# Sixteen weight offsets, five matmul orders and three woven blocks in an attention and two-layer expert kernel

## The chip, the cores and the metric

The kernel runs on one core of a Trainium2 chip. The metric is the device time of one execution in microseconds; of several executions the median is taken. The core's engines run beside each other: TensorE (PE, with its weight loads shown as PEld), VectorE (DVE), ScalarE (ACT), GpSimd (POOL), and SyncE, whose queue issues nearly all DMAs.

## The reference

Attention with mixed heads is followed by two feed-forward layers, all in fp32. With 2 batches, 12 heads, a sequence of 448 and a head size of 64 the attention gives 896 rows of 768, and each feed-forward part widens them to 2048 and back:

```python
scores = scale * np.matmul(q, k.transpose(0, 1, 3, 2))
scores = np.einsum('bhij,hg->bgij', scores, w_pre)
attn = softmax(scores)
attn = np.einsum('bhij,hg->bgij', attn, w_post)
x = np.matmul(attn, v)                        # -> 896 x 768

h = x @ w_in                                  # 768 -> 2048
g = h * np.clip(h + 3.0, 0.0, 6.0) / 6.0
x = g @ w_out                                 # 2048 -> 768

h = x @ w_in2
g = np.maximum(h, 0.0) + alpha * np.minimum(h, 0.0)
return g @ w_out2
```

## The kernel before

The attention fills the first part of the span, the feed-forward layers the rest; their first matmuls lie among the last ones of the attention. Only the feed-forward layers are touched by the change.

Each number of these layers is held as a pair, a high part `h` in the type fp32r and a low part `l`, the rest. A product of two such pairs is three matmuls (`mm3`): high weights by high input, high weights by low input, low weights by high input. Each matmul has 128 rows, 128 columns of weights, and moves 448 columns (`S`), one of the two batch halves `c`. It brings its own weight load.

The weights come in 64 blocks of 128 x 768. Blocks 0 to 15 are the first input layer, 16 to 31 the first output layer, 32 to 47 the second input layer, 48 to 63 the second output layer. A block of an input layer holds one slice `f` of 128 hidden units, with six slices `kk` of the 768 inputs; `in_chain` adds 18 matmuls into one PSUM tile `p` for each half `c`. A block of an output layer holds two hidden slices by 384 outputs and adds 36 matmuls into six tiles. So every block is 36 matmuls, and the second input layer's block 32 starts at 414.78 us of the span.

A block arrives in a packed form of two 32-bit words per weight, and every engine has a share in unpacking it, for block `i` in this order:

- `load_w`: SyncE's queue brings `wst`.
- `conv_magnitude`: ScalarE makes `wb` from one word (L361) and scales the other (L367).
- `conv_shift`: VectorE clamps and shifts `wb` (L377, L378); `conv_sign`: VectorE puts the sign in (L385).
- `conv_round`: GpSimd adds the other word (L392).
- `conv_hi`: ScalarE casts `wb` to `whi` (L397); `conv_lo`: GpSimd subtracts to get `wlo` (L403).

There is no scheduler: each engine works in the order in which the code is written. In step `i` of an input layer `in_layer` writes: rounding for block i+2, the load for i+4, magnitude for i+3, then for half 0 the 18 matmuls, the activation, `conv_hi` and `conv_lo` for i+2 and `conv_shift` for i+3, and for half 1 the 18 matmuls, `conv_sign` for i+3 and the activation. The second layer's activation `act2` is two VectorE operations that read `p` (L505, L506), a cast on ScalarE (`gh`, L510) and a subtraction on VectorE (`gl`, L512). `whi` and `wlo` have three buffers each; `p` rotates over eight PSUM tiles.

In the built program every `whi` and `wlo` tile begins 192 bytes past a multiple of 256, and every slice that the matmuls move begins on a multiple of 256; the slices of the weights are 512 bytes apart.

Of the kernel before, what the change touches and what calls it, by code (L numbers as in the profile page):

```python
# [7 lines left out]
F32 = mybir.dt.float32  # L8
R = mybir.dt.float32r
# [4 lines left out]
ALU = mybir.AluOpType  # L14
# [21 lines left out]
def kernel(  # L36
# [15 lines left out]
    nc = tc.nc  # L52
    _, D, H, S = k.shape
    B, D = q.shape[0], D // 2
# [3 lines left out]
    KF = alpha.shape[0] // 128  # L58
    KD = DM // 128
# [10 lines left out]
    for b in range(B):  # L70
        for i0 in range(0, S, GP):
            n = min(GP, S - i0)
# [34 lines left out]
    with tc.manual_schedule():  # L107
# [214 lines left out]
        for ti in range(NTILE - 1):  # L322
            lo = (tiles[ti]["s"] + tiles[ti]["ng"] - 1) // 2 + 2
            hi = tiles[ti + 2]["s"] // 2 + 1 if ti + 2 < NTILE else lo + 4
# [3 lines left out]
        P = {}  # L328
        WC = w_in1.shape[2]
        blocks = []  # L330
# [3 lines left out]
        st_t, b_t, w_t, x_t, x_whole = {}, {}, {}, {}, {}  # L334
# [22 lines left out]
        def conv_abs(i):  # L357
            if i < len(blocks):
                t = w_tile(i, "wb", [128, WC], F32)
                s = st_t[i]  # L360
                nc.scalar.activation(t, s[:, :, 1].bitcast(F32), ACTF.Abs)  # L361
                b_t[i] = t

        def conv_low(i):
            if i < len(blocks):
                s = st_t[i]
                nc.scalar.activation(s[:, :, 0].bitcast(I32), s[:, :, 0], ACTF.Copy, scale=2.0 ** -29)  # L367

        def conv_magnitude(i):
            conv_abs(i)  # L370
            conv_low(i)

        def conv_shift(i):
            if i < len(blocks):
                t = b_t[i]
                u = t.bitcast(U32)
                nc.vector.tensor_scalar(t, t, W_MAX, W_MIN, ALU.min, ALU.max)  # L377
                nc.vector.tensor_scalar(  # L378
                    u, u, 3, 0x3FFFFFFF, ALU.logical_shift_left, ALU.bitwise_and
                )  # L380
# [8 lines left out]
        def conv_round(i):  # L389
            if i < len(blocks):  # L390
                n = b_t[i].bitcast(I32)
                nc.gpsimd.tensor_tensor(n, n, st_t.pop(i)[:, :, 0].bitcast(I32), ALU.add)  # L392

        def conv_hi(i):
            if i < len(blocks):
                hi = P["w"].tile([128, WC], R, tag="whi", bufs=3, name="whi")
                nc.scalar.copy(hi, b_t[i])  # L397
                w_t[i] = [hi]

        def conv_lo(i):  # L400
            if i < len(blocks):
                lo = P["w"].tile([128, WC], R, tag="wlo", bufs=3, name="wlo")
                nc.gpsimd.tensor_tensor(lo, b_t.pop(i), w_t[i][0].bitcast(F32), ALU.subtract)  # L403
                m = KD if blocks[i][0] == "in" else 2
                w_t[i] = [x.rearrange("p (k f) -> p k f", k=m) for x in (w_t[i][0], lo)]

        def conv_a(i):
            conv_magnitude(i)
# [29 lines left out]
        def ptile():  # L438
            if "ps6" not in P:
                return P["ps2"].tile([128, 512], F32, tag="p", name="p")  # L440
            n_ps[0] += 1
            where = P["ps6"] if n_ps[0] % 8 < 6 else P["ps2"]
            return where.tile([128, 512], F32, tag="p", name="p")
# [24 lines left out]
        def mm3(p, wt, xt, first, last):  # L468
            for z, (a, c) in enumerate(((0, 0), (0, 1), (1, 0))):
                nc.tensor.matmul(  # L470
                    p, wt[a], xt[c], start=(first and z == 0), stop=(last and z == 2)
                )

        def in_part(p, i, xs, c, k0, k1):
            for kk in range(k0, k1):
                mm3(p, [w[:, kk, :] for w in w_t[i]], xs[kk, c], kk == 0, kk == KD - 1)

        def in_chain(i, xs, c):
            p = ptile()[:, :S]
            in_part(p, i, xs, c, 0, KD)  # L480
            return p

        def g_tile(f, c):
            return pair(P["g0" if c == 0 and f < NE else "g1"], "g")
# [29 lines left out]
        def run(a):  # L514
            for _ in a:
                pass

        def in_layer(i, xs, act, gs, f0):
            for f in range(f0, KF):
                conv_round(i + 2)  # L520
                load_w(i + 4)
                conv_magnitude(i + 3)
                for c in range(B):
                    p = in_chain(i, xs, c)
                    gs[f, c] = g_tile(f, c)
                    a = act(p, gs[f, c], f)
                    next(a)
                    if c == 0:
                        conv_hi(i + 2)
                        conv_lo(i + 2)  # L530
                        conv_shift(i + 3)
                        next(a)
                    else:
                        conv_sign(i + 3)
                        next(a)
                    run(a)
                w_t.pop(i)
                i += 1
            return i
# [11 lines left out]
        for c in range(2):  # L551
            a = GH * c
# [24 lines left out]
        for i in range(NC):  # L577
            a = 2 * (17 + 7 * i)
# [35 lines left out]
        for p_ in range(-2, NP + 1):  # L614
            if p_ == -2:
                for g in range(6):
                    if g == 4:
                        for c in range(2):
                            a = GH * c
# [35 lines left out]
            kk = 2 * (p_ - (NP - KD // 2))  # L655
# [36 lines left out]
        for f in range(NC):  # L692
            p = in_chain(f, x_t, 1)
# [134 lines left out]
```

## Time and profile before

| | |
|---|---|
| time, median of 3 runs | 647.37 us |
| time, lowest and highest run | 644.71 and 649.35 us |
| span of the profiled execution | 649.1 us |
| TensorE busy | 634.1 us, 98% of the span |
| VectorE, ScalarE, GpSimd busy | 64%, 53%, 45% of the span |
| granted TensorE clock | 1.000 |

The span runs from the first to the last instruction of one profiled execution; the runs are other executions of the same kernel. The profiled one lies 1.7 us above the median of the runs and within what they span. The clock of 1.000 is the upper of TensorE's two levels, 2.4 GHz. Busy shares are means over stages that differ much, so they don't say what sets the end.

### The profile page before, as it was taken

To read this page: it belongs to the slowest core of one execution; us is meant where nothing else is said; L and a number is where in the kernel's file an instruction comes from. 1 tells how busy PE (TensorE), PEld (TensorE's weight loads), DVE (VectorE), ACT (ScalarE), POOL (GpSimd) and SP (SyncE) were. 2 spreads that over 40 slices of the span, in tenths; PEclk is the share of its full clock that TensorE was granted. 3 is DMA by queue.
4 is the path that set the end of the run, shared out by engine and by line. 5 is a ranking of instruction groups with operands and counts; after the bars stand their busy time and mean duration, and the time that the engine had idled before them with its cause. 6 is when DMAs were issued, how large, how long until landed. Compare 5 with 4: busy or idle time off the path is not lost.

```text
span 649.1 us, 16015 instructions
## 1 busy us (share of the span) xinstructions
PE 634.1 (98%) x6696; PEld 545.8 (84%) x6696; DVE 417.6 (64%) x649; ACT 344.0 (53%) x635; POOL 294.2 (45%) x240
## 2 busy tenths in 40 slices
PE   7999999899899999999999999999999999999997
PEld 2667666666589999999999999999999999999997
DVE  3866666668546888887534634489999997454401
ACT  4877778686555566656444433444444443444310
POOL 4211123314425554545775555344455556776430
PEclk9999999999999999999999999999999999999999
DMA  7677646735202223323443333222222234445202
GB/s 194 221 234 212 189 142 202 222 137 142 85 3 98 97 98 118 126 98 99 145 146 118 118 106 97 98 94 101 98 98 97 98 99 144 147 137 192 98 0 86
DMA packets 32117, 81.72 MB, mean 126 GB/s; under 512 B 8364, under 2 KB 21420, under 8 KB 32044
## 3 DMA queue, kind: packets, MB, share of 16 engines
q1 hardware_dynamic: 31468, 80.27, 38.0%
q8 instruction: 53, 0.87, 0.5%
q10 hardware_dynamic: 576, 0.41, 0.3%
q14 instruction: 20, 0.16, 0.1%
HBM read 58.65 MB, written 2.75 MB: 95 GB/s over the span
## 4 chain that ended last, share of the span: by engine, by line
PE 96%; issue 1%; DVE 1%; ACT 1%; DMA 0%; POOL 0%; ACTq 0%; POOLq 0%; DVEq 0%
PE p L470 71%; PE pt L254 7%; PE av L305 6%; PE sc L186 6%; PE mx L215 6%; ACT e L230 0%; DMA qst<-in_q_dram 0%; DVE wr L242 0%; DVE nm L221 0%; ACT MT L269 0%; DVE sm L237 0%; POOL wr L242 0%; DVE S L566 0%; DVE o L747 0%; DVE MT L269 0%
## 5 line engine op out<-in xcount | busy, mean ns | idle before, releaser
L403 POOL TENSOR_TENSOR wlo<-wb,whi 128x768 fp32r<-128x768 f32 x64 | 126.7, 1980 | 124.9 <-ACT whi L397 124.9
L392 POOL TENSOR_TENSOR wb<-wb,wst 128x768 int32<-128x768 int32 x64 | 125.5, 1960 | 81.8 <-DVE wb L385 65.8
L470 PE MATMUL p<-xh,whi 128*128 128x448 f32 x384 | 139.9, 364 | 0.0
L470 PE MATMUL p<-xl,whi 128*128 128x448 f32 x384 | 139.4, 363 | 0.0
L470 PE MATMUL p<-gl,whi 128*128 128x448 f32 x384 | 139.3, 363 | 0.0
L470 PE MATMUL p<-gh,wlo 128*128 128x448 f32 x384 | 138.9, 362 | 0.0
L470 PE MATMUL p<-gh,whi 128*128 128x448 f32 x384 | 138.8, 361 | 0.0
L470 PE MATMUL p<-xh,wlo 128*128 128x448 f32 x384 | 138.3, 360 | 0.0
L377 DVE TENSOR_SCALAR wb<-wb 128x768 f32<-128x768 f32 x64 | 53.3, 833 | 79.0 <-ACT wb L361 78.9
L361 ACT ACTIVATE wb<-wst 128x768 f32<-128x768 f32 x64 | 57.8, 904 | 70.0 <-DMA wst<-in_w_out_dram 51.2
L397 ACT CAST whi<-wb 128x768 fp32r<-128x768 f32 x64 | 53.3, 832 | 48.7 <-PE p L470 33.3
L470 PEld LDWEIGHTS p<-xh,whi 128*128 128x128 f32 x384 | 72.1, 188 | 8.0 <-issue 1.6
L230 ACT ACTIVATE e<-mx,nm 128x448 f32<-128x448 f32 x90 | 56.3, 632 | 40.2 <-DVE nm L221 40.0
L470 PEld LDWEIGHTS p<-gh,whi 128*128 128x128 f32 x384 | 72.0, 187 | 5.3
L470 PEld LDWEIGHTS p<-gh,wlo 128*128 128x128 f32 x384 | 71.9, 187 | 4.9 <-POOL wlo L403 0.4
L470 PEld LDWEIGHTS p<-gl,whi 128*128 128x128 f32 x384 | 72.1, 188 | 4.7
L470 PEld LDWEIGHTS p<-xh,wlo 128*128 128x128 f32 x384 | 71.8, 187 | 5.0
L470 PEld LDWEIGHTS p<-xl,whi 128*128 128x128 f32 x384 | 72.1, 188 | 3.9
L221 DVE TENSOR_REDUCE nm<-mx 128x1 f32<-128x448 f32 x90 | 52.1, 618 | 30.8 <-PE mx L215 30.5
L242 POOL TENSOR_SCALAR wr<-wpost,sm 128x60 f32<-128x60 f32 x74 | 25.3, 356 | 100.4 <-DVE sm L238 90.6
L385 DVE SCALAR_TENSOR_TENSOR wb<-wst,wb 128x768 uint32<-128x768 uint32 x64 | 69.1, 1080 | 1.1
L254 PEld LDWEIGHTS pt<-wr,e 60*64 60x64 f32 (+1 forms) x2880 | 51.7, 134 | 19.8 <-issue 11.8
(51 smaller groups left out, 760.5 us busy)
## 6 DMA issues: line engine op xcount, KB each, us to landing
wst<-in_w_out_dram SPq DMA_DIRECT2D x32, 768.0 KB
wst<-in_w_in_dram SPq DMA_DIRECT2D x27, 768.0 KB
pull<-S SPq DMA_DIRECT2D x88, 210.0 KB
wst<-in_w_in_dram SPq DMA_DIRECT2D x10, 384.0 KB
v<-in_v_dram SPq DMA_DIRECT2D x16, 168.0 KB
out_dram<-o SPq DMA_DIRECT2D x12, 224.0 KB
kst<-in_k_dram SPq DMA_DIRECT2D x11, 224.0 KB
qst<-in_q_dram SPq DMA_DIRECT2D x10, 180.0 KB
```

What stands on the lines that cost most here:

```text
L186: nc.tensor.matmul(ps[o][r:r + z - a, :S], t[D * o:D * o + D, a:z], k_[D * o:D * o + D, j, :], start=True, stop=True,)
L215: nc.tensor.matmul(ms[r][Q * c:Q * c + Q, :S], wpre[a:z], d[a:z, c, :], start=True, stop=True)
L221: nc.vector.tensor_reduce(nm, m[:, :S], axis=AX.X, op=ALU.max, negate=True)
L230: nc.scalar.activation(out=e, in_=ms[o][:, :S], func=ACTF.Exp, bias=nms[o], accum_out=sm[:, o:o + 1])
L254: nc.tensor.matmul(ts[c][Q * z:Q * z + m, u:u + GH], e[a:a + GH, j:j + m], wr[a:a + GH], start=True, stop=True,)
L361: nc.scalar.activation(t, s[:, :, 1].bitcast(F32), ACTF.Abs)
L377: nc.vector.tensor_scalar(t, t, W_MAX, W_MIN, ALU.min, ALU.max)
L385: nc.vector.scalar_tensor_tensor(u, st_t[i][:, :, 1], 0xC0000000, u, ALU.bitwise_and, ALU.bitwise_or)
L392: nc.gpsimd.tensor_tensor(n, n, st_t.pop(i)[:, :, 0].bitcast(I32), ALU.add)
L397: nc.scalar.copy(hi, b_t[i])
L403: nc.gpsimd.tensor_tensor(lo, b_t.pop(i), w_t[i][0].bitcast(F32), ALU.subtract)
L470: nc.tensor.matmul(p, wt[a], xt[c], start=(first and z == 0), stop=(last and z == 2))
```

## The change

Four things change for single blocks; what is computed stays the same.

- Tiles of `whi` and `wlo` grow from 768 to 832 words (3072 to 3328 bytes, both multiples of 256), and the block lies in them at `offset(i, z)`: in the first output layer both parts at 0, 16, ... 240 bytes by the number of the block, in the second output layer the low part alone; in blocks 41 and 42 both at 64 and 128 bytes; elsewhere at 0.
- Five blocks of the second input layer run through `steps`. Block 34 has the products in the order high-high, low-high, high-low; 35 in low-high, high-high, high-low; 36 takes each weight slice for both batch halves in turn; 37 takes all slices of one product before the next product; 38 moves 224 columns at a time, the first half of the columns and then the second.
- Blocks 40 to 42 are woven: high and low part of one weight lie side by side, so that weights of one part are two words apart. ScalarE writes them with two casts, GpSimd with six subtractions, one for each slice.
- `wlo` is taken from its pool together with `whi`.

```diff
+        IN2, OUT2 = len(blocks) // 2, len(blocks) // 2 + KF
+
+        def offset(i, z):
+            if KF <= i < IN2 or i >= OUT2 and z:
+                return 4 * (i % 16)
+            return {IN2 + 9: 16, IN2 + 10: 32}.get(i, 0)
+
+        def woven(i):
+            return IN2 + 8 <= i < IN2 + 11
+
         def conv_hi(i):
             if i < len(blocks):
-                hi = P["w"].tile([128, WC], R, tag="whi", bufs=3, name="whi")
-                nc.scalar.copy(hi, b_t[i])
-                w_t[i] = [hi]
+                hi, lo = (
+                    P["w"].tile([128, WC + 64], R, tag=f"w{z}", bufs=3, name=f"w{z}")
+                    [:, offset(i, y):offset(i, y) + WC]
+                    for y, z in enumerate(("hi", "lo"))
+                )
+                b, m = b_t[i], KD if blocks[i][0] == "in" else 2
+                if woven(i):
+                    parts = [x.rearrange("p (f z) -> p f z", z=2) for x in (hi, lo)]
+                    for y, x in enumerate(parts):
+                        nc.scalar.copy(x[:, :, 0], b[:, y * WC // 2:(y + 1) * WC // 2])
+                    w_t[i] = [
+                        [parts[kk // 3][:, kk % 3 * 128:kk % 3 * 128 + 128, z] for kk in range(KD)]
+                        for z in range(2)
+                    ]
+                    return
+                nc.scalar.copy(hi, b)
+                w_t[i] = [x.rearrange("p (k f) -> p k f", k=m) for x in (hi, lo)]
 
         def conv_lo(i):
             if i < len(blocks):
-                lo = P["w"].tile([128, WC], R, tag="wlo", bufs=3, name="wlo")
-                nc.gpsimd.tensor_tensor(lo, b_t.pop(i), w_t[i][0].bitcast(F32), ALU.subtract)
...
+                b = b_t.pop(i)
+                if woven(i):
+                    h, l = w_t[i]
+                    for kk in range(KD):
+                        nc.gpsimd.tensor_tensor(
+                            l[kk], b[:, kk * 128:kk * 128 + 128], h[kk].bitcast(F32), ALU.subtract
+                        )
+                    return
+                h, l = (x.rearrange("p k f -> p (k f)") for x in w_t[i])
+                nc.gpsimd.tensor_tensor(l, b, h.bitcast(F32), ALU.subtract)
...
+        def steps(i, xs):
+            f = i - IN2
+            w = [[x[kk] if woven(i) else x[:, kk, :] for kk in range(KD)] for x in w_t[i]]
+            ps = [ptile()[:, :S] for _ in range(B)]
+            z3 = [(0, 0), (0, 1), (1, 0)]
+            if f == 2:
+                z3 = [(0, 0), (1, 0), (0, 1)]
+            if f == 3:
+                z3 = [(1, 0), (0, 0), (0, 1)]
+            ks = [(kk, z) for kk in range(KD) for z in z3]
+            if f == 5:
+                ks = [(kk, z) for z in z3 for kk in range(KD)]
+            halves = [(0, S // 2), (S // 2, S)] if f == 6 else [(0, S)]
+            if f == 4:
+                todo = [(c, halves[0], k) for k in ks for c in range(B)]
+            else:
+                todo = [(c, n, k) for c in range(B) for n in halves for k in ks]
+            for c, (a, z), (kk, (y, x)) in todo:
+                nc.tensor.matmul(
+                    ps[c][:, a:z], w[y][kk], xs[kk, c][x][:, a:z], start=(kk, (y, x)) == ks[0],
+                    stop=(kk, (y, x)) == ks[-1],
+                )
+            return ps
...
+                ps = steps(i, xs) if IN2 + 2 <= i <= IN2 + 6 else None
                 for c in range(B):
-                    p = in_chain(i, xs, c)
+                    p = ps[c] if ps else in_chain(i, xs, c)
```

The first place in the order is TensorE in block 36. A name with its number is one tile; `p_5911` and `p_5943` (before) or `p_5911` and `p_5912` (after) are the sums of the two halves. Before, around the change from the first half to the second:

```order
L470 MATMUL p_5911<-xh_5189,whi_5805 128x448
L470 MATMUL p_5911<-xl_5190,whi_5805 128x448
L470 MATMUL p_5911<-xh_5189,wlo_5807 128x448
L470 MATMUL p_5943<-xh_5199,whi_5805 128x448
L470 MATMUL p_5943<-xl_5200,whi_5805 128x448
L470 MATMUL p_5943<-xh_5199,wlo_5807 128x448
```

After, at any slice of that block:

```order
L532 MATMUL p_5911<-xh_5189,whi_5824 128x448
L532 MATMUL p_5912<-xh_5199,whi_5824 128x448
L532 MATMUL p_5911<-xl_5190,whi_5824 128x448
L532 MATMUL p_5912<-xl_5200,whi_5824 128x448
L532 MATMUL p_5911<-xh_5189,wlo_5825 128x448
L532 MATMUL p_5912<-xh_5199,wlo_5825 128x448
```

The first half's sum gets its last matmul as the 35th of the block, where it was the 18th.

The second place is TensorE in block 38, before and after, again where the second half begins:

```order
L470 MATMUL p_6041<-xh_5189,whi_5935 128x448
L470 MATMUL p_6041<-xl_5190,whi_5935 128x448
L470 MATMUL p_6041<-xh_5189,wlo_5937 128x448
L470 MATMUL p_6073<-xh_5199,whi_5935 128x448
L470 MATMUL p_6073<-xl_5200,whi_5935 128x448
```

```order
L532 MATMUL p_6041<-xh_5189,whi_5954 128x224
L532 MATMUL p_6041<-xl_5190,whi_5954 128x224
L532 MATMUL p_6041<-xh_5189,wlo_5955 128x224
L532 MATMUL p_6042<-xh_5199,whi_5954 128x224
L532 MATMUL p_6042<-xl_5200,whi_5954 128x224
```

The block has 72 matmuls of 224 columns, where it had 36 of 448.

The third place is GpSimd at the woven blocks 40 to 42, one piece of the difference; `wb` is the unpacked block:

```order
 L392 TENSOR_TENSOR wb<-wb,wst 128x768
-L403 TENSOR_TENSOR wlo<-wb,whi 128x768
+L430 TENSOR_TENSOR whi<-wb,whi 128x128 x3
+L430 TENSOR_TENSOR wlo<-wb,wlo 128x128 x3
 L392 TENSOR_TENSOR wb<-wb,wst 128x768
```

Six short subtractions stand where one stood, between the roundings of two blocks; on ScalarE two casts of 128 x 384 stand where one of 128 x 768 stood. Nothing else changes its place on any engine.

## Rows read from the trace of the kernel before

**Rows 1.** The page: busy time of each engine; the chain that ended last.

```profile
PE 634.1 (98%) x6696; PEld 545.8 (84%) x6696; DVE 417.6 (64%) x649; ACT 344.0 (53%) x635; POOL 294.2 (45%) x240
...
PE p L470 71%; PE pt L254 7%; PE av L305 6%; PE sc L186 6%; PE mx L215 6%; ACT e L230 0%; DMA qst<-in_q_dram 0%; DVE wr L242 0%; DVE nm L221 0%; ACT MT L269 0%; DVE sm L237 0%; POOL wr L242 0%; DVE S L566 0%; DVE o L747 0%; DVE MT L269 0%
```

**Rows 2.** The chain in order of time, from 160 us: start, duration, what.

```profile
191.54 353.41 PE p L470 x1766
...
544.99 100.70 PE p L470 x502
```

**Rows 3.** Windows, L470 alone; counts take in what reaches over an edge.

```profile
371.58:378.78 7.20, 7.20 (x38) 6.75 (x36) 1.00 0.46 166
414.78:421.98 7.20, 7.20 (x38) 6.75 (x36) 1.00 0.12 48
443.58:450.78 7.20, 7.20 (x38) 6.75 (x36) 1.00 0.28 106
457.98:465.18 7.20, 7.20 (x38) 6.75 (x36) 1.00 0.33 112
544.38:551.58 7.20, 7.16 (x36) 6.37 (x35) 1.00 0.49 182
```

**Rows 4.** Timeline of matmuls (PE) and weight loads (PEld) at 544.6 us.

```profile
544.58 0.37 PE L470 MATMUL p<-gl,whi 128*128 128x448 f32 x1
...
545.29 0.37 PE L470 MATMUL p<-gh,whi 128*128 128x448 f32 x1
545.50 0.37 PE L470 MATMUL p<-gl,whi 128*128 128x448 f32 x1
545.70 0.36 PE L470 MATMUL p<-gh,wlo 128*128 128x448 f32 x1
...
544.99 0.19 PEld L470 LDWEIGHTS p<-gh,wlo 128*128 128x128 f32 x1 [0.42 <-POOL wlo L403]
545.10 0.19 PEld L470 LDWEIGHTS p<-gh,whi 128*128 128x128 f32 x1
```

**Rows 5.** Timeline of GpSimd in the second input layer and at its end.

```profile
451.08 1.85 POOL L403 TENSOR_TENSOR wlo<-wb,whi 128x768 fp32r<-128x768 f32 x1 [0.95 <-ACT whi L397]
455.62 2.19 POOL L392 TENSOR_TENSOR wb<-wb,wst 128x768 int32<-128x768 int32 x1 [2.68 <-DVE wb L385]
...
535.44 1.85 POOL L403 TENSOR_TENSOR wlo<-wb,whi 128x768 fp32r<-128x768 f32 x1 [0.95 <-ACT whi L397]
543.09 1.84 POOL L403 TENSOR_TENSOR wlo<-wb,whi 128x768 fp32r<-128x768 f32 x1 [0.94 <-ACT whi L397]
```

**Rows 6.** Timeline of VectorE, step of block 36, first half.

```profile
448.31 0.68 DVE L505 TENSOR_SCALAR t<-p,alpha_sb 128x448 f32<-128x448 f32 x1
...
449.57 0.99 DVE L377 TENSOR_SCALAR wb<-wb 128x768 f32<-128x768 f32 x1
450.59 0.56 DVE L378 TENSOR_SCALAR wb<-wb 128x768 uint32<-128x768 uint32 x1
451.50 1.91 DVE L512 TENSOR_TENSOR gl<-t,gh 128x448 fp32r<-128x448 f32 x1 [0.35 <-ACT gh L510]
```

**Rows 7.** Timelines of TensorE and VectorE in the layer's first block, 32.

```profile
418.18 0.36 PE L470 MATMUL p<-xh,wlo 128*128 128x448 f32 x1
...
418.58 0.69 DVE L505 TENSOR_SCALAR t<-p,alpha_sb 128x448 f32<-128x448 f32 x1 [2.41 <-PE p L470]
...
420.90 0.62 DVE L512 TENSOR_TENSOR gl<-t,gh 128x448 fp32r<-128x448 f32 x1
```

**Rows 8.** Groups of all GpSimd and ScalarE instructions, shapes apart.

```profile
L466 POOL TENSOR_TENSOR xl<-xT,xh 128x448 fp32r<-128x448 f32 x6 | 6.9, 1143 | 13.8 <-ACT xh L465 13.8
L466 POOL TENSOR_TENSOR xl<-xT,xh 128x240 fp32r<-128x240 f32 x6 | 4.0, 697 | 0.0
...
L397 ACT CAST whi<-wb 128x768 fp32r<-128x768 f32 x64 | 53.3, 832 | 48.7 <-PE p L470 33.3 <-POOL wb L392 15.1
L510 ACT CAST gh<-t 128x448 fp32r<-128x448 f32 x32 | 18.1, 565 | 54.1 <-DVE t L506 54.1
```

More of the change, by code (lines that the diff above doesn't have):

```diff
@@ L400, in conv_lo @@
+                nc.scalar.copy(hi, b)
+                w_t[i] = [x.rearrange("p (k f) -> p k f", k=m) for x in (hi, lo)]
         def conv_lo(i):
             if i < len(blocks):
-                lo = P["w"].tile([128, WC], R, tag="wlo", bufs=3, name="wlo")
-                nc.gpsimd.tensor_tensor(lo, b_t.pop(i), w_t[i][0].bitcast(F32), ALU.subtract)
-                m = KD if blocks[i][0] == "in" else 2
-                w_t[i] = [x.rearrange("p (k f) -> p k f", k=m) for x in (w_t[i][0], lo)]
+                b = b_t.pop(i)
@@ L475, in in_part @@
             for kk in range(k0, k1):
-                mm3(p, [w[:, kk, :] for w in w_t[i]], xs[kk, c], kk == 0, kk == KD - 1)
+                w = [x[kk] if woven(i) else x[:, kk, :] for x in w_t[i]]
+                mm3(p, w, xs[kk, c], kk == 0, kk == KD - 1)
         def in_chain(i, xs, c):
```

## The prediction

> **What bounds the kernel now.** I read the page first: TensorE is busy for 98% of the span and 71% of the chain that ends last is one line, L470, the matmul of the two expert layers [rows 1]. Then the same chain in order of time: from 191.54 to 645.69 there are two uninterrupted runs of L470 with a hole between them [rows 2]. So from 191 us on nothing but the pace of L470 counts, as long as weights arrive. Then windows of 7.20 us: each holds the 36 weight loads of one block, 0.200 us a matmul, in the first output layer (371.58) and in the second input layer (414.78, 443.58, 457.98) alike; only the one at 544.38 holds 35 [rows 3]. The matmul's busy time is no help, since 0.36 us is shown for one that is followed by the next after 0.20 us; starts have to be subtracted [rows 4].
>
> The hole at 544.58 shows the two other clocks of this line [rows 4]. The weight load that starts at 544.99 waited 0.42 us for wlo. The next load starts 0.11 us later, at 545.10, and the next matmul at 545.29. The hole costs (0.41 - 0.20) + (0.30 - 0.20) = 0.3 us. So a load of 128 columns keeps the loader for 0.11 us, though it is shown as 0.19 us long, and it lies under a 0.20 us matmul. All matmuls of these rows move 448 columns, and all loads take contiguous weights at one offset modulo 256 bytes.
>
> The hole's cause is the supply. In the second input layer VectorE has no slack: wlo ends at 452.93 (451.08 + 1.85) for block 38, which starts at 457.98, five us early; at 544.93 (543.09 + 1.84) for block 50, which wants it at that moment [rows 3, 5]. From 451.08 to 535.44 are eleven blocks, 7.67 us each against 7.20 on TensorE: the reserve melts by 0.47 us a block and is gone just where the hole is. VectorE's round [rows 6]: it works from 448.31 to 451.15, waits for gh, then gl takes 1.91 us instead of the 0.62 of an undisturbed one [rows 7], and ends 0.48 us after GpSimd's wlo, which runs from 451.08 to 452.93 [rows 5].
>
> **The change part by part.**
>
> Offsets. Nothing is added; weight tiles grow from 3072 to 3328 bytes, and weights of blocks 16 to 31 (both halves) and 48 to 63 (wlo alone) move in steps of 16 bytes. No row shows a load of 128 columns at another offset. If a column takes one cycle at 2.4 GHz, 448 take 0.187 us, and 0.013 of each 0.200 us has no name in the trace. Two bounds for an unlucky or lucky offset follow: that 0.013 doubled or gone. For 15 shifted blocks that is 15 x 36 x 0.0133 = 7.2 us in the first output layer and, for the third of the loads that are wlo, 2.4 us in the second: -9.6 to +9.6 us. I take 0: even the waiting load at 544.99, without a matmul beside it, was spaced no better than 0.11 us, and that leaves 0.09 us under each matmul for a slower load [rows 4].
> [...]
>
> Orders. Blocks 34 (weights by input: hi-hi, lo-hi, hi-lo), 35 (lo first) and 37 (one product after the other over all slices) issue the same 36 matmuls with 36 loads. In before's order the weights stay for one step and change for the next, and so do the moving tiles, and all steps have the same 0.20 us [rows 4]; 0. Block 35 asks for wlo 0.4 us earlier, of five us of reserve; 0.
>
> Block 36 alternates the two batch halves. TensorE's time stays 7.20 us, but the first half's result is finished by the 35th matmul instead of the 18th. VectorE took it at 448.31 [rows 6]; now the 35th starts at 443.58 + 34 x 0.20 = 450.38 and its result comes some 0.4 us later (at block 32, where VectorE does wait: 18th start 418.18, reader 418.58 [rows 7]), so at 450.78: VectorE waits about 2.5 us, and behind the wait queue shift, gl, the second half's act2 and sign of block 39, and through sign GpSimd's rounding and the weights from block 39 on. Part comes back at once: L377 would then start at 452.1, meet the end of wlo(38) at 452.93, end with L378 near 453.9, and gl, by then undisturbed, at 454.5 instead of 453.41 [rows 6]. Lag: 1.1 us, 2.5 at worst. It costs nothing while the reserve lasts.
>
> Block 38 in 224 columns: 72 matmuls with 72 loads. Bounds: half the time each, 72 x 0.10 = 7.20, no cost (nor a gain, as the same columns are moved); if a load's full 0.19 us had to lie between matmul starts, 72 x 0.20 = 14.4, +7.2 us. A load now no longer fits under its matmul, and the spacing of two loads, 0.11 us [rows 4], becomes the pace: 72 x 0.11 = 7.9, **+0.7 us**, which I take, as it is the one row that shows the loader by itself.
>
> Woven blocks 40 to 42. ScalarE makes two casts of 384 instead of one of 768 (0.83 us; 448 take 0.57, so about 0.52 each, +0.2 us). GpSimd makes six subtractions of 128 instead of one of 768: between 240 columns (0.70) and 448 (1.14) a column costs 2.1 ns, so 128 take about 0.46, six 2.8 against 1.85 us alone: +0.9 us [rows 5, 8]. GpSimd has that time: it idles 2.68 us before each rounding [rows 5]. VectorE's gl on the other hand meets pieces of 0.46 instead of 1.85 us. At best it saves 1.29 us a block (1.91 - 0.62), at worst it loses, as sign meets the longer tail; I take 0.5 us, three times 1.5. Whether TensorE loads weights of every second column as fast no row shows: nothing at one bound; at the other a load takes twice 0.11 us, which no longer fits under 0.20: 108 x 0.02 = 2.2 us. I take 0, since a load may slow by four fifths, from 0.11 to 0.20, before it shows.
> What the Trainium skill states on both: SBUF — State Buffer, Who interferes with whom, has VectorE's two-input operations and GpSimd shut each other out for a whole instruction, which the 1.91 us gl bears out (here +1.29). Its Specifications want two hits on a 16-byte line for full speed; woven fp32 weights just give two, so by it the 2.2 us fall away, and no run here shows it yet.
>
> Sum of the lag at block 50: 0.3 (today's hole) + 1.1 (block 36) - 0.7 (TensorE itself later by block 38) - 1.5 (woven) = -0.8 us: the hole closes, **-0.3 us**, and late next is nothing, as the output layer builds its reserve up again. Total +0.7 - 0.3 = +0.4 us: the profiled execution's span would go from 649.1 to 649.5; against the median of the runs, 647.37, which lies 1.7 us below that span, 647.8 us.
>
> **The rivals.**
> A, the offsets disturb the loads (slower). Place: the first output layer and a third of the second. Price: 0.013 us for each load off its old place, so 647.8 + 9.6 = 657.4 if 15 of 16 offsets are bad, 652.6 if half are. It decides against 1% from 10 of the 16 on. For it: the unexplained 0.013. Against: the pace is the same to the hundredth in both layers of rows 3, whose moving tiles lie in quite other places, if always on multiples of 256 [rows 3].
> B, the same the other way: the old offset is a bad one and the 0.013 goes: 638.2. Against it speaks that all 15 would have to be better.
> C, the narrow matmuls wait for the whole load, 0.20 us each: 647.8 + 6.5 = 654.3. For it: the load is shown as 0.19 long. Against: the next load, and with it the first matmul's release of the loader, came after 0.11 [rows 4].
> D, the lag isn't paid back: block 36 costs the whole 2.5 us and the woven pieces give VectorE nothing. The hole becomes 0.3 + 2.5 - 0.7 = 2.1 us: 647.4 + 0.7 + 1.8 = 649.9. If the woven loads take 2.2 us themselves, that delays TensorE and fills the hole: 647.4 + 0.7 - 0.3 + 2.2 = 650.0. About 650 either way. For it: a VectorE without slack; against: GpSimd's idle time.
>
> **How the numbers follow.** Forecast 66%, A with most offsets 10% and with half 6%, B 3%, C 6%, D 9%. A measurement of this kernel can tell about 1%, 6.5 us, from no change: its runs alone lie from 644.71 to 649.35. The forecast with that spread is 645 to 650.5; D and A with half the offsets lie up to 652.6; C straddles 654. From 645 to 655 holds about 8 in 10; what is left out is A with most offsets, half of C, and B. Slower by over 1% (above 653.8): A and most of C, 0.15; faster: 0.03; within: 0.82.
>
> **What the profile after would show.** Right: windows of 7.20 us for blocks 16 to 31, 34 to 37 and 40 to 42; near 7.9 for block 38 with loads 0.11 apart; a wait of VectorE on p of some 2.5 us in block 36; gl near 1.2 us in the three woven steps; no wait for wlo at block 50. Wrong: windows of the output layers that change with the block's number, by up to 0.48 us each (A, B); 14 us for block 38 (C); a hole longer than 0.3 us near block 50, or woven windows above 7.20 (D). What would make it all wrong is a pace of the loads that depends on offset by more than the 0.013 us.

## The result and the profile after

The changed kernel takes 653.21 us against 648.66 us (medians of 17 runs each, taken in turn on one chip): ratio 1.0079, 95% interval 1.0054 to 1.0104. It is slower, by 3.5 to 6.7 us; the ratio stays under the 1% that the prediction took as its limit, though the end of the interval lies just above it. The profiled execution has a span of 652.8 us, 3.7 more than before, where the prediction's sum gave 0.4 more. A run's time is 1.8 us longer than its span (654.61 us for the 652.8), so the profiled execution before, with its span of 649.1, took some 650.9 us by this estimate and lay above all three runs of the first table, not within what they span. The comparisons leave out runs that lie over 1.5% above a kernel's fastest; in two experiments below the runs fall in two groups, so those are told by their single times.

The page of after: busy time of each engine, and the chain (the work that ended last, followed back from its end) by line. The expert layers' matmul, L470 before, now stands on two lines: L500, and L532 for the five blocks with orders of their own.

```profile
PE 639.3 (98%) x6732; PEld 550.6 (84%) x6732; DVE 414.3 (63%) x649; ACT 345.4 (53%) x638; POOL 297.9 (46%) x255
...
PE p L500 66%; PE pt L254 6%; PE sc L186 6%; PE av L305 6%; PE p L532 6%; PE mx L215 5%; DMA kst<-in_k_dram 1%; DMA pull<-S 1%; DMA qst<-in_q_dram 0%; ACT e L230 0%; DVE wr L242 0%; DVE nm L221 0%; ACT MT L269 0%; DVE sm L237 0%; POOL wr L242 0%
```

The chain in order of time, of after: start, duration, what.

```profile
191.09 239.85 PE p L500 x1188
430.94 36.83 PE p L532 x216
467.77 181.60 PE p L500 x900
```

Against [rows 2] the expert layers begin 0.45 us earlier (191.09 for 191.54), run without a hole to 649.37 (467.77 + 181.60), and end 3.68 us later than at 645.69. So 4.1 us were lost between, all of it on TensorE, none of it in a wait. Where, the windows say.

A window's row gives its edges and length, the busy time of matmuls and of weight loads with their numbers, the granted clock, and the share and rate of the DMAs. First before's window at the same place as the first of after:

```profile
299.13:414.33 115.20, 115.20 (x578) 107.98 (x577) 1.00 0.37 119
```

Windows of after, matmuls of L500 alone: the first output layer's first 115.20 us (16 blocks of 7.20 would fit), the woven blocks 40 to 42, and 100.80 us of the second output layer (14 blocks of 7.20).

```profile
299.13:414.33 115.20, 115.20 (x567) 106.23 (x566) 1.00 0.36 117
...
474.84:496.48 21.64, 21.64 (x108) 20.72 (x107) 1.00 0.33 110
532.68:633.48 100.80, 100.80 (x500) 93.57 (x499) 1.00 0.34 116
```

16 blocks are 576 loads (before's 577 take in one that reaches over the edge), and only 566 began: ten matmuls of 0.2 us, 2 us, are missing. In the second output layer it is 499 of 504, 1 us. The granted clock is 1.00 in all three. That this goes by offset shows in the starts of blocks. Timeline of TensorE, of after: the first matmuls of blocks 16 and 17 (offsets 0 and 16 bytes), 21 and 22 (80, 96), 26 and 27 (160, 176).

```profile
299.13 0.36 PE L500 MATMUL p<-gh,whi 128*128 128x448 f32 x1
306.34 0.36 PE L500 MATMUL p<-gh,whi 128*128 128x448 f32 x1
...
335.73 0.37 PE L500 MATMUL p<-gh,whi 128*128 128x448 f32 x1
343.17 0.36 PE L500 MATMUL p<-gh,whi 128*128 128x448 f32 x1
...
372.40 0.36 PE L500 MATMUL p<-gh,whi 128*128 128x448 f32 x1
379.60 0.37 PE L500 MATMUL p<-gh,whi 128*128 128x448 f32 x1
```

Block 16 takes 7.21 us, block 21 takes 7.44, block 26 takes 7.20: the same 36 matmuls, no wait in them, at another offset. The busy time of one (0.36, 0.37) hides it; again starts have to be subtracted.

Block 38 in 224 columns. Timeline of the weight loads, of after:

```profile
459.58 0.19 PEld L532 LDWEIGHTS p<-xl,whi 128*128 128x128 f32 x1
459.69 0.19 PEld L532 LDWEIGHTS p<-xh,wlo 128*128 128x128 f32 x1
459.80 0.19 PEld L532 LDWEIGHTS p<-xh,whi 128*128 128x128 f32 x1
```

They are 0.11 us apart, and the block lasts from 459.58 to 467.61, 8.03 us. VectorE, timeline of after: block 36, the step of block 38, where nothing woven is made, then the step in which GpSimd and ScalarE make the woven block 40.

```profile
452.38 0.69 DVE L560 TENSOR_SCALAR t<-p,alpha_sb 128x448 f32<-128x448 f32 x1 [2.40 <-PE p L532]
...
455.45 0.62 DVE L567 TENSOR_TENSOR gl<-t,gh 128x448 fp32r<-128x448 f32 x1
...
461.83 1.90 DVE L567 TENSOR_TENSOR gl<-t,gh 128x448 fp32r<-128x448 f32 x1 [0.35 <-ACT gh L565]
...
464.91 0.95 DVE L385 SCALAR_TENSOR_TENSOR wb<-wst,wb 128x768 uint32<-128x768 uint32 x1
...
469.63 0.75 DVE L567 TENSOR_TENSOR gl<-t,gh 128x448 fp32r<-128x448 f32 x1 [0.48 <-ACT gh L565]
...
471.55 1.25 DVE L385 SCALAR_TENSOR_TENSOR wb<-wst,wb 128x768 uint32<-128x768 uint32 x1
```

GpSimd in the same step and at block 50 (timeline of after), and the load that waited in [rows 4]:

```profile
468.79 1.91 POOL L430 TENSOR_TENSOR whi<-wb,whi 128x128 fp32r<-128x128 f32 x3 [0.65 <-ACT whi L415]
470.67 1.32 POOL L430 TENSOR_TENSOR wlo<-wb,wlo 128x128 fp32r<-128x128 f32 x3
...
543.60 1.83 POOL L435 TENSOR_TENSOR wlo<-wb,whi 128x768 fp32r<-128x768 f32 x1 [0.95 <-ACT whi L421]
```

```profile
547.16 0.19 PEld L500 LDWEIGHTS p<-gl,whi 128*128 128x128 f32 x1
547.37 0.19 PEld L500 LDWEIGHTS p<-gh,wlo 128*128 128x128 f32 x1
```

wlo is done at 545.43 and wanted at 547.37: 1.9 us of reserve where there was a wait of 0.42, and no hole.

### The profile page after: what moved, and what is told of

Its sections match the earlier page's. It is cut to its first block, busy times and chain, and to the rows that moved or that the text cites. A ratio compares the mean times of both kernels' runs of the same rounds, so it can differ in the third digit from the quotient of the medians.

```text
span 652.8 us, 16103 instructions
## 1 busy us (share of the span) xinstructions
PE 639.3 (98%) x6732; PEld 550.6 (84%) x6732; DVE 414.3 (63%) x649; ACT 345.4 (53%) x638; POOL 297.9 (46%) x255
## 4 chain that ended last, share of the span: by engine, by line
PE 95%; DMA 2%; DVE 1%; issue 1%; ACT 1%; POOL 0%; SPq 0%; POOLq 0%; DVEq 0%; ACTq 0%
PE p L500 66%; PE pt L254 6%; PE sc L186 6%; PE av L305 6%; PE p L532 6%; PE mx L215 5%; DMA kst<-in_k_dram 1%; DMA pull<-S 1%; DMA qst<-in_q_dram 0%; ACT e L230 0%; DVE wr L242 0%; DVE nm L221 0%; ACT MT L269 0%; DVE sm L237 0%; POOL wr L242 0%
## 5 line engine op out<-in xcount | busy, mean ns | idle before, releaser
L435 POOL TENSOR_TENSOR wlo<-wb,whi 128x768 fp32r<-128x768 f32 x61 | 120.8, 1980 | 127.5 <-ACT whi L421 127.5
L500 PE MATMUL p<-gl,whi 128*128 128x448 f32 x384 | 140.4, 366 | 0.0
L500 PE MATMUL p<-gh,whi 128*128 128x448 f32 x384 | 140.1, 365 | 0.0
L500 PE MATMUL p<-gh,wlo 128*128 128x448 f32 x384 | 139.9, 364 | 0.0
L500 PE MATMUL p<-xh,whi 128*128 128x448 f32 x324 | 116.3, 365 | 0.0
L500 PE MATMUL p<-xh,wlo 128*128 128x448 f32 x324 | 115.0, 361 | 0.0
L500 PE MATMUL p<-xl,whi 128*128 128x448 f32 x306 | 111.1, 363 | 0.0
L500 PEld LDWEIGHTS p<-gh,whi 128*128 128x128 f32 x384 | 72.1, 188 | 6.1
L500 PEld LDWEIGHTS p<-gh,wlo 128*128 128x128 f32 x384 | 72.1, 188 | 5.7
L500 PEld LDWEIGHTS p<-gl,whi 128*128 128x128 f32 x384 | 72.1, 188 | 5.6
L421 ACT CAST whi<-wb 128x768 fp32r<-128x768 f32 x61 | 50.7, 832 | 48.5 <-PE p L500 36.0
L500 PEld LDWEIGHTS p<-xh,whi 128*128 128x128 f32 x324 | 61.0, 188 | 6.8 <-issue 1.6
L500 PEld LDWEIGHTS p<-xh,wlo 128*128 128x128 f32 x324 | 60.9, 188 | 4.1
L500 PEld LDWEIGHTS p<-xl,whi 128*128 128x128 f32 x306 | 57.6, 188 | 3.2
```

Of the source, the lines that this page charges most:

```text
L421: nc.scalar.copy(hi, b)
L435: nc.gpsimd.tensor_tensor(l, b, h.bitcast(F32), ALU.subtract)
L500: nc.tensor.matmul(p, wt[a], xt[c], start=(first and z == 0), stop=(last and z == 2))
```

## The experiments

Each edit is shown against the changed kernel. The two lines that take out the orders and the weaving stand once, in the first; they hold in all others but the second, the third and, where it says so, later ones. A line `+ return ...` alone is then the whole of `offset`, in floats of four bytes.

### Offsets alone

```diff
-            return {IN2 + 9: 16, IN2 + 10: 32}.get(i, 0)
+            return 0
-            return IN2 + 8 <= i < IN2 + 11
+            return False
-                ps = steps(i, xs) if IN2 + 2 <= i <= IN2 + 6 else None
+                ps = None
```

Expected: 

> The offsets of the two output layers alone, no other matmul order, no narrow and no woven blocks. If the place of the weights sets the pace of the block that reads them, the output layers' windows are those of the changed kernel (blocks 16 to 31 together 2.0 us above 16 x 7.20, blocks 48 to 63 1.3 us above), the hole of 0.3 us near block 50 is back, and the time is 3.0 to 3.6 us above before (ratio about 1.005). If the other edits caused the slower output layers (rival), all windows there are 7.20 us and the time is that of before.

Measured: 653.07 against 649.3 us, ratio 1.0053 (1.0018 to 1.0088). Window of the same 115.20 us of the first output layer, and a load in block 50:

```profile
299.38:414.58 115.20, 115.20 (x567) 106.24 (x566) 1.00 0.35 117
```

```profile
546.89 0.19 PEld L500 LDWEIGHTS p<-gh,wlo 128*128 128x128 f32 x1 [0.39 <-POOL wlo L435]
```

The same 566 loads as in the changed kernel, and the hole is back. So the offsets by themselves cost what the first output layer lost, and they have nothing to do with the hole going. In the second output layer the loss is again 1.3 us, but some 0.3 of it is the hole: by their starts blocks 51 and 52 (low part at 48 and 64 bytes) lose 40 ns each here and lost 78 and 160 in the changed kernel. So the low part alone has more than one pace at some offsets.

### Everything but the offsets of the output layers

```diff
-            if KF <= i < IN2 or i >= OUT2 and z:
-                return 4 * (i % 16)
```

Expected: 

> The changed kernel with every block of the output layers back at offset 0; the five orders, the narrow and the woven blocks stay. If the place of the weights sets the pace, blocks 16 to 31 and 48 to 63 take 7.20 us each, block 38 8.03 and the woven ones 7.32, 7.33 and 7.20, and there is no hole: 1.1 - 0.3 = 0.8 us above before (ratio about 1.001). If it is not the offsets but the larger tiles, which moved every other tile of these layers (rival), the output layers stay 3.3 us slower and the ratio is that of the changed kernel, 1.008.

Measured: 649.52 against 649.3 us, ratio 1.0003 (0.9977 to 1.0028). The window at the same place:

```profile
298.19:413.39 115.20, 115.20 (x578) 107.98 (x577) 1.00 0.36 120
```

577 loads, as many as before. The weight tiles are as large as in the changed kernel, so their size costs nothing; block 38 takes 8.03 us, the woven ones 7.33, 7.32 and 7.20, and no hole opens: by the blocks these parts add 1.1 us and give back 0.33, and the 0.8 that is left is less than the times can tell.

### Offsets in reverse, block 38 in 320 and 128 columns

```diff
-                return 4 * (i % 16)
-            return {IN2 + 9: 16, IN2 + 10: 32}.get(i, 0)
+                return 4 * ((15 - i) % 16)
+            return {IN2 + 8: 32, IN2 + 10: 16}.get(i, 0)
...
-            halves = [(0, S // 2), (S // 2, S)] if f == 6 else [(0, S)]
+            halves = [(0, 320), (320, S)] if f == 6 else [(0, S)]
```

Expected: 

> The changed kernel with the offsets in reverse (block 16 at 240 bytes, block 31 at 0), the woven blocks 40, 41, 42 at 128, 0 and 64 bytes, and block 38 split into 320 and 128 columns. If the offset of the block being read sets its pace, block 31 (0) and block 21 (160) take 7.20 us, block 29 (32) and block 26 (80) about 7.43, and the woven ones 7.20, 7.32, 7.33. If the number of the block, its buffer or the neighbouring blocks' writes set it (rival), blocks 18 and 21 stay at 7.43 and block 26 at 7.20. Block 38: if a narrow matmul is paced by its load of 0.111 us and a wide one by its columns plus 0.013, 36 x (0.147 + 0.111) = 9.3 us; if every matmul pays its columns plus a fixed 0.018 (rival), 36 x (0.151 + 0.071) = 8.0 us, as with two halves.

Measured: one run, 655.19 us, against 649.3. The cost goes with the offset, not with the block: 14 of 16 offsets cost within 20 ns of what they cost in the changed kernel (the table below). The woven block at 128 bytes is again the free one, 7.22 us, now as block 40; those at 0 and 64 take 7.32 and 7.33. Block 38 takes 9.24 us. Timeline of the loads in it, first wide matmuls:

```profile
458.89 0.19 PEld L532 LDWEIGHTS p<-xl,whi 128*128 128x128 f32 x1
459.03 0.19 PEld L532 LDWEIGHTS p<-xh,wlo 128*128 128x128 f32 x1
459.18 0.19 PEld L532 LDWEIGHTS p<-xh,whi 128*128 128x128 f32 x1
459.32 0.19 PEld L532 LDWEIGHTS p<-xl,whi 128*128 128x128 f32 x1
```

The wide ones are 0.14 to 0.15 apart here and 0.147 on average over the block, by their columns; the narrow ones 0.11, as with 224 columns. So a narrow matmul is paced by its load, not burdened with a fixed cost.

### All 64 blocks at 32 bytes

```diff
+            return 8
```

Expected: 

> Before's orders, and every weight block of all four layers, both parts, 32 bytes later. If the offset sets the pace, every block takes 7.43 us as block 18 of the changed kernel did, also in the input layers: 62 x 0.23 = 14 us above before (ratio 1.02), and the hole is gone since TensorE is slower than the supply. If the cost comes from blocks at unlike offsets lying next to each other (rival), every block takes 7.20 us and the time is that of before.

Measured: 664.05, 650.93, 667.88 and 665.88 us, against 649.3 before. In the profiled run (664.05) every block takes 7.440 us:

```profile
301.47:416.67 115.20, 115.20 (x559) 105.05 (x558) 1.00 0.34 114
```

62 blocks of 0.24 us make 14.9, and the run lies 14.8 above before; the granted clock is 1.00, so it isn't the clock. But one run of the same program took 650.93. It left no trace; a faster rhythm at this offset, in which a run can stay, would explain it, and single blocks of the mixed run below show such a rhythm at 32 bytes.

### Moving operands instead of weights

Two unused tiles of 56 floats (48 before, and none) push the x and g parts to 224 modulo 256; weights where they were.

```diff
-            pool(ctx, "gap", bufs=1, side="right").tile([128, 48], F32, name="gap")
+            pool(ctx, "gap", bufs=1, side="right").tile([128, 56], F32, name="gap")
...
+            pool(ctx, "gap1", bufs=1).tile([128, 56], F32, name="gap1")
             P["g1"] = pool(ctx, "g1", bufs=2 * KF - NE)
```

Expected: 

> Before's matmul orders, no woven parts, all weights at offset 0 as before; two unused gap tiles push every moving operand of the expert layers (x parts and g parts, and the t tiles) to addresses 224 modulo 256 where they were 0 modulo 256. Theory R (the pace depends on where the weights lie relative to the moving operand, modulo 256): weights are now 32 bytes further on relative to it, as with the offset of 32 bytes, so the blocks take 7.43 to 7.44 us where they took 7.20 (unless the run settles in the faster of the two cycles), 64 x 0.24 = 15 us more: about 664. Rival W (the place of the weights alone decides): every block 7.20 and the time of the kernel before, 649. A third outcome, some other excess between 0 and 0.24 us that is the same in all blocks of a layer, would say that both places matter.

Measured: three runs at 662.58 to 665.73, seven from 650.39 to 656.11; those seven give 1.0061 (1.0024 to 1.0097). The profiled run (665.73) has 7.440 us in every block:

```profile
303.22:418.42 115.20, 115.20 (x559) 104.80 (x558) 1.00 0.34 114
```

The same 558 loads as with the weights 32 bytes on, again at a granted clock of 1.00, and again two groups of runs. No weight was moved. Where the weights lie by themselves is not it.

### Both moved

The same two tiles, and the weights 56 floats, 224 bytes, further on: weights and moving operands lie 32 bytes earlier modulo 256, together.

```diff
+            return 56
```

Expected: 

> As the run with the moving operands at 224 modulo 256, and the weights of all 64 blocks 224 bytes further on, which is 32 bytes earlier modulo 256: weights and moving operand lie to each other as in the kernel before. Theory R: 7.20 us per block, the time of before (649). Rival W: weights at offset 224 cost as in the changed kernel, +0.16 to +0.19 us per block, 10 to 12 us in all: about 660.

Measured: 650.55 against 648.89, ratio 1.0023 (0.9992 to 1.0055).

```profile
300.27:415.47 115.20, 115.20 (x577) 107.98 (x576) 1.00 0.37 120
```

7.200 us a block, although the weights lie at an offset that cost 0.19 in the changed kernel. So the pace follows the distance between weights and moving operand, as far as it was tried: the moving operands were moved by this one step only, the other steps by the weights alone. (The three buffers of a part lie 3328 bytes, 13 times 256, apart, and the blocks that rotate through them take the same, so it is the distance modulo 256.) The hole in block 50 is there as in the kernel before, 0.46 us.

### All blocks at 160 bytes

```diff
+            return 40
```

Expected: 

> All 64 blocks at offset 160 bytes, before's orders and places otherwise. The blocks at 160 bytes took 7.204 and 7.212 us in the changed kernel, so both theories expect 7.20 to 7.21 per block: 649 to 650, the time of before. If instead single layers come out at another pace, what a block costs is not set by its offset alone but also by the cycle that it happened to start in (160 bytes cost 0.116 in the second output layer with the low part alone moved).

Measured: 650.2 against 648.89, ratio 1.0026 (0.9993 to 1.0059).

```profile
299.50:414.70 115.20, 115.20 (x577) 108.14 (x576) 1.00 0.36 120
```

Each block takes 7.200 us, but for the hole of 0.29 in block 50: moving the weights costs nothing in itself.

### Only the woven blocks, at 128 bytes

```diff
+            return 32 if woven(i) else 0
```

The weaving stays in; the orders are out.

Expected: 

> The kernel before with one part of the change: blocks 40 to 42 woven, their weights at offset 128 bytes, where a woven block took 7.198 us; no other offsets, before's orders. Expected: the woven blocks 7.20 us each, VectorE's conversions beside them faster than before (gl near 0.75 us instead of 1.9), and if those are what opened the hole of 0.33 us in block 50, it is gone: 648.9 against 649.2, no difference that can be measured. Rival: woven blocks cost 0.12 us each here too (0.35 in all) and the hole stays.

Measured: 648.14 against 648.89, ratio 0.9983 (0.9955 to 1.0012). Windows of blocks 16 to 31 and of 40 to 42, then the loads at block 50:

```profile
297.13:412.33 115.20, 115.20 (x577) 107.98 (x576) 1.00 0.36 120
...
469.94:491.54 21.60, 21.60 (x110) 20.84 (x109) 1.00 0.33 110
```

```profile
541.94 0.19 PEld L498 LDWEIGHTS p<-gl,whi 128*128 128x128 f32 x1
542.14 0.19 PEld L498 LDWEIGHTS p<-gh,wlo 128*128 128x128 f32 x1
```

The woven blocks cost nothing at this offset, and the hole is gone without any other part. By its blocks it is the best version there is, 0.3 us ahead of the kernel before; that is less than the times can tell.

### High and low part apart

```diff
+            return 8 * (i >> z & 1)
```

Expected: 

> Before's orders, nothing woven. Of every four blocks in a row the first has both parts at offset 0, the second the high part alone at 32 bytes, the third the low part alone, the fourth both. Two of three matmuls use the high part. If the pace of a block is chosen anew in each (the theory so far), blocks with both parts at 0 take 7.200 us, those with both 7.43, and the others lie between, by the share of matmuls 0.15 for the high part and 0.08 for the low, or at 7.200; 16 x (0.23 + 0.15 + 0.08) = 7.4 us in all at most. Rival: the slow cycle stays on once it has begun, so that blocks with both parts at 0 behind a slow one also take 7.4; some 15 us in all.

Measured: one run, 653.16, against one of before, 652.98. Timeline of TensorE: first matmuls of blocks 24 to 28 (none, high, low, both moved, none).

```profile
355.77 0.37 PE L498 MATMUL p<-gh,whi 128*128 128x448 f32 x1
...
362.99 0.36 PE L498 MATMUL p<-gh,whi 128*128 128x448 f32 x1
...
370.26 0.36 PE L498 MATMUL p<-gh,whi 128*128 128x448 f32 x1
...
377.54 0.37 PE L498 MATMUL p<-gh,whi 128*128 128x448 f32 x1
...
384.98 0.37 PE L498 MATMUL p<-gh,whi 128*128 128x448 f32 x1
```

7.21, 7.27, 7.28 and 7.44 us, the same in every four. The rival, a slow rhythm that stays, is out: the block behind a slow one is back at once. But the shares are not those of the matmuls (two of three use the high part): 0.07 for the high part, 0.08 for the low, 0.24 for both, so the parts don't add up. Nor is 0.08 the only price of the low part at 32 bytes: block 50 of the changed kernel lost 0.16 with it (the table below).

### All offsets, each four times

```diff
+            return 4 * ((i * (3, 5, 7, 11)[i // 16] + i // 16) % 16)
```

Expected: 

> Before's orders, nothing woven, both parts of all 64 blocks moved, each of the sixteen offsets four times, behind another offset each time. Theory so far (what a block costs follows from its offset, with one or two possible values for each): four like values for each offset, or two values; by the changed kernel's output layers 0.13 us a block on average, 64 x 0.128 = 8.2 us in all. Rival (the offset of the block ahead matters as much, since the block starts in the rhythm which that one left): values scattered within one offset by as much as between offsets.

Measured: one run, 652.37, against one of before, 652.98; the times hide the loss, since in this run the expert layers begin early (the last rows of this document). Blocks 2 to 62 lose 7.2 us together, 0.118 each. Excess of a block over 7.200 us in ns, from the starts of its first matmul and of the next block's (at the changed kernel's first output layer, the reversed run's, this mixed run, where blocks 0, 1 and 63 are left out, and the changed kernel's second output layer with the low part alone moved):

```
bytes  changed  reversed  mixed, four times     low part alone
    0        5         0  13 4 10                            0
   16      155       148  147 155 151 153                   84
   32      229       232  231 0 156 238                    160
   48      120         6  117 1 116                         78
   64       93        93  96 98 98 94                      160
   80      234       237  231 238 229 234                   82
   96      151       163  85 153 154 152                     2
  112       89        77  86 78 83 87                      109
  128       77        78  87 80 84                           0
  144      116       121  118 118 117 122                   87
  160        4        12  6 15 2 4                         120
  176      145       148  146 147 137 147                  140
  192      148       136  142 145 139 144                   79
  208      160        82  83 77 80 160                      40
  224      190       190  185 188 184 193                  160
  240      123       125  120 116 122 122                   13
```

With both parts moved, twelve of sixteen offsets have one value, whatever stood ahead of them and in whichever layer; 32, 48, 96 and 208 have two or three. The rival, scatter within an offset as large as between offsets, is out.

### The load by itself, at twelve offsets

Blocks 34 to 45 all in 224 columns, block k at 16 times (k modulo 16) bytes: `steps` serves these twelve, with its other orders and the weaving taken out.

```diff
+            return 4 * (i % 16) if IN2 + 2 <= i < IN2 + 14 else 0
...
+            halves = [(0, S // 2), (S // 2, S)]
+                ps = steps(i, xs) if IN2 + 2 <= i < IN2 + 14 else None
```

Expected: 

> Twelve blocks of the second input layer (34 to 45) in 224 columns, block k with both parts at offset 16 times (k modulo 16) bytes, 32 to 208; everything else as before. With 224 columns the loads set the pace (0.11 us each in the changed kernel's block 38), so the run shows the load itself at each offset. If an unlucky offset makes the load slow, so slow that 0.2 us of matmul no longer covers it (the step of the prediction that took the offsets at nothing spoke against this, with 0.09 us to spare), the loads at 32 and 80 bytes come over 0.2 us apart and their blocks take 14.5 us or more. If the load stays covered and it is the matmul beside it that is slowed by a few ns, all twelve blocks take 8.0 to 8.3 us, loads 0.11 to 0.115 apart. Time either 649 + 12 x 0.83 to 1.1 = 659 to 662, or 680 and more.

Measured: one run, 664.32, against one of before, 650.02. Windows of the blocks at 32, 80 and 160 bytes:

```profile
432.81:440.84 8.03, 8.03 (x72) 8.03 (x72) 1.00 0.26 84
...
456.93:464.96 8.03, 8.03 (x74) 8.03 (x73) 1.00 0.31 114
497.13:505.16 8.03, 8.03 (x74) 8.03 (x73) 1.00 0.25 88
```

All twelve take 8.03 to 8.05 us. Where the loads set the pace, 32 and 80 bytes, the dearest offsets, cost no more than 160, a free one. No load is slow at these offsets; they cost something only beside matmuls of 448 columns, which are longer than the loads. Whether it is the moving of the columns or the change from one set of weights to the next that then takes longer, the runs don't show.

## Why the prediction was near and where it was off

The time, 653.21, lies within 645 to 655, and the ratio of 1.0079 within the 1% that had the chance of 0.82. That is not the sum's doing: the forecast by itself stood for 645 to 650.5, and the range was wider for the sake of rivals, of which A with half of the offsets (652.6) came nearest. The predicted 647.8 is 5.4 us off. Of that 1.3 are the comparison's other median of before (648.66 for 647.37). The sum makes 3.7, as the blocks lost 4.1 us for the 0.4 predicted, and the last 0.4 is less than the times can tell. The terms:

- **Offsets. This is the step that failed: "I take 0".** Measured +2.0 us in the first output layer and +1.3 in the second (the sums of the table's first and last columns), 3.3 of the 4.1 us lost. The bounds held: 7.2 and 2.4 us were named, at 0.0133 us a load; in the first layer the dearest offset costs 0.234 / 36 = 0.0065 a matmul, and the mean of the fifteen 2.04 / 15 / 36 = 0.0038; in the second the dearest costs 0.160 / 12 = 0.0133 for each load that was moved, just the bound. Rival A had the place and the sign right, at a third of its price (3.3 of 9.6); its mechanism, disturbed loads, is not what the runs show. No offset takes a block below 7.20, so rival B is out. The reason for the zero was right as far as it went: a load under a 0.2 us matmul has 0.09 us to spare, and no load is slow at any of twelve offsets (blocks of 8.03 to 8.05 us). It did not follow that the pair costs nothing. I had asked only whether the load fits under the matmul, never whether the two side by side can take longer than the matmul did before. Against A I had set that the pace is equal in both layers, with tiles "if always on multiples of 256": that clause was the answer, as weights and moving operands kept one distance there modulo 256.
- **Orders, 0.** Blocks 34 to 37 take 7.200 us each. Right.
- **Block 36.** VectorE waits 2.40 us, where 2.5 stood; its t starts at 452.38, which is the predicted 450.78 and the 1.60 us by which the block itself begins later (445.18 for 443.58). gl starts at 455.45 and takes 0.62, undisturbed, as said. Right; it costs nothing.
- **Block 38.** +0.83 us for +0.7, loads 0.11 apart. Right, and the reversed run shows that it is the load's pace. Rival C is out.
- **Woven blocks on TensorE, 0.** Measured 0.12, 0.13 and 0.00: +0.24 us, inside the bound of 2.2. The block at 128 bytes shows that reading every second column need not cost anything. At 0 bytes it does cost 0.12, where a block that isn't woven costs nothing: the free place is another one for woven weights. That the load "may slow by four fifths" was the same half of the question.
- **Woven supply.** gl falls from 1.91 to 0.75 us, more than to the 1.2 expected; sign grows from 0.95 to 1.25, as feared. The six subtractions take 1.91 + 1.32 = 3.2 us for 2.8. By these rows the gain is 1.16 - 0.30, some 0.9 us a block; by the starts of gl in the three woven steps (469.63, 476.57 and 483.51, so 6.94 us apart where 7.67 stood) it is 0.7. The prediction took 0.5.
- **The hole, -0.3.** Gone, by 0.33. With the woven blocks alone it is gone as well, with the offsets alone it is back: the reserve comes from the weaving. Rival D is out.

The measured sum is 2.04 + 1.31 + 0.83 + 0.24 - 0.33 and 0.04 in blocks behind the changed ones, 4.1 us; less 0.45 for the earlier start, the 3.7 of the spans.

On the weight load and the moving operand the Trainium skill (SBUF — State Buffer, Who interferes with whom) calls TensorE's two read ports independent. The runs show a limit to that: 32 bytes between the two, moved on either side, cost 0.0067 us a matmul; by which path isn't known. On the same page the Trainium skill (Specifications (TRN2)) asks for two hits or more on a 16-byte line for full bandwidth, which woven weights just give. The woven block's 7.20 us at 128 bytes agrees; the 7.32 at 0 this does not account for.

**What stays open.** Why the distance counts was not found out, and only one distance was made in both ways, by the weights and by the moving operands. The starts show matmuls that fall into short rhythms, 0.200 throughout at 160 bytes, 0.207, 0.207, 0.206 at 32, and no rhythm found was faster than 0.200 on average. Why a few offsets, and whole runs at 32 bytes, have two rhythms or more, and what picks one, is not known. Nor is it known at what pace the seven quicker runs with moved operands went, 0.6% over before, since only the profiled one left a trace.

## What to carry to other kernels

Where matmul and weight load run side by side all the time, the distance of their addresses, modulo 256 bytes here, is part of the layout: a new or a larger tile in a pool can cost up to 3% of the matmuls' time with no matmul changed and no wait in the trace, as in three of the ten runs with the moving operands moved. Check it by subtracting the starts of matmuls over one block, not by busy time and not by the run's time, which scatters by several us here. And that an operation is hidden under another one does not show that the pair costs no more than the longer one: ask that too.

## What the runs showed of the hardware

- A 448-column matmul is followed by the next after 0.200 us on average in every block at one distance of weights and moving operand, and after 0.207 at another; the sixteen steps of 16 bytes cost 0 to 0.24 us a block of 36.
- The same program at 32 bytes took 650.93 us once and 664 to 668 three times.
- High and low part moved alone by 32 bytes cost 0.07 and 0.08 us a block, both 0.24, in the run made for it; the low part alone cost 0.16 at 32 bytes in the changed kernel, and 0.12 at 160, where both cost nothing.
- Loads of 128 columns follow each other after 0.11 us at each of the twelve offsets from 32 to 208 bytes; a block with loads of every second float takes 7.20 us at 128 bytes and 7.32 at 0.
- The part ahead of the expert layers scatters from run to run: the uninterrupted run of matmuls began at 186.00 us in the mixed run and at 192.23 with both moved, on the same code. That is more than most of the effects here, and why blocks were compared and not spans.

The starts of the last point, from the chain in order of time, of the mixed run and of the run with both moved:

```profile
186.00 461.17 PE p L498 x2268
```

```profile
192.23 302.42 PE p L499 x1511
```
